# RWKV attention and a mixture of experts on one core: sends one step sooner, two more units transposed by TensorE, blank rows from ScalarE's queue

## Chip, cores and metric

One core of a Trainium2 chip. The metric is the device time of one launch, in microseconds, as the median of several runs. TensorE multiplies matrices, VectorE and ScalarE work on tiles, GpSimd does products between tiles in SBUF and issues indirect DMAs, and SyncE (SP) issues most of the plain DMAs and all transposing ones. Each engine works through its own instructions in order.

## The reference

Two parts, the second on the output of the first:

```python
for t in range(S):                     # batch 4, heads 8, S 768, head_dim 48
    kt, vt, rt = (k[:, :, t], v[:, :, t], r[:, :, t])
    cur = np.einsum('bhd,bhe->bhde', u[None] * kt, vt)
    y[:, :, t] = np.einsum('bhd,bhde->bhe', rt, state + cur)
    state = w[None, :, :, None] * state + np.einsum('bhd,bhe->bhde', kt, vt)
...
x = y.transpose(0, 2, 1, 3).reshape(3072, 384)
logits = x @ w_gate + modality_bias[modality_id]      # 8 experts
e_idx = np.argmax(logits, axis=1)
gate_w = softmax(logits)[np.arange(N), e_idx]
for e in range(8):
    mask = e_idx == e
    out[mask] = gate_w[mask, None] * (np.maximum(x[mask] @ w1[e], 0.0) @ w2[e])
```

w1 is 384 x 1024 for each expert, w2 is 1024 x 384. Every token goes to one expert.

## The kernel before

**Units and steps.** The attention is cut into 24 units of 128 tokens (4 batches by 6 chunks of the sequence). Step i of the big loop in `run` (L1239) does the attention of unit i and prepares its neighbours: `scores` of unit i + 1 (r times k, L451), `values` of unit i (L479, L486) with the state's update (L501), `token`, `factor`, `high` and `low` of unit i - 1 (the output as a pair of 16-bit halves in the tile `row`), and the keys (`kc`), decays (`rc`), `kt` and r-times-k products (`rk`, from unit 14 on `ru`) of units i + 2 and i + 3. In the code, VectorE's `keys` writes `kc`, GpSimd's `decay` writes `rc` (L377), `carry` writes `kt` (L384), `own_keys` writes `ru` (L390, L391); VectorE's `taken` sums `ru` at the unit's own step (L422).

**Routing.** Units form seven groups (`GROUPS`: 0 to 3, 4 to 7, 8 to 11, 12 to 15, 16 to 18, 19 to 21, 22 and 23). For each group: the rows are transposed (`flip`) into `xT`; two steps after the group's last unit `logits` multiplies them by the gate (six matmuls for each unit, L591); `choose` takes the expert, `count` and `place` give each token a row in its expert's region of the DRAM table `rows`, and `send` writes the rows there with one indirect DMA for each unit (L681, with a one-element memset before each). `choose`, `place` and `ahead` are generators that are worked off a piece at a time wherever the loop calls `fill`. `route(i, d, f)` calls f for the group whose last unit is d steps back.

**Transposing.** `flip` has two ways. For units 0 to 7 (`TURNED`) and for the last, TensorE transposes six 128 x 128 tiles into PSUM (L577) and ScalarE copies them to `xT` (`flipped`, L581). For the others SP issues a transposing DMA (L572), and TensorE waits for it at the logits.

**Slots.** The expert that is expected to be the fullest is begun while the attention runs: ten slots of 128 rows of it. `turn` reads a slot's rows from `rows` with a transposing DMA into `mxT` (L1027) and a small one (L1028); it waits for every send that was issued before it. `s_up` multiplies by w1 (`phs`, L1040), `s_high` and `s_low` make the 16-bit halves `hh` and `hl`, `s_down` multiplies by w2 (`pos`, L1114, L1119), `s_take` and `s_give` write the result. In the loop, slots 0 to 5 go up at steps 11, 13, 15, 17, 19 and 21 (`ups`) and down one step later; their turns are issued at the end of steps 9, 10, 13, 14, 17 and 18, turns 6 and 7 at the end of steps 21 and 22 (`turns`). Slots 6 to 9 follow after the loop in an order written out by hand. After the slots a loop goes through the other experts' rows.

**Blank rows.** `fronts` (L298) writes 128 rows of zeros at the front of each expert's region, 1544 KB in one DMA. It is called at the end of step 22, ahead of turn 7, and issued by SP.

**PSUM.** `scores`, the transposes of `flip`, `s_up` and `s_down` take tiles in turn from one ring of four (`ps_a`).

**Order on GpSimd.** In each step: `send` of two units of the group six steps back, `own_keys`, `decay`, `send` of two more, `s_give`, `carry`, `sign` (L1309 to L1317). SP's order in a step: the loads of k and v (L357), r (L365) and of the transposed r and k (L348) for later units, then `flip`, then a piece of the second expert's weights (L942) or a `turn`.

Of the kernel before, what the change touches and what calls it, by code (L numbers as in the profile page):

```python
# [45 lines left out]

TURNED = 7

# [16 lines left out]
class _Kernel:  # L65
# [225 lines left out]

    def blank(self, rows, of):
        i = self.nc.sync.dma_start(rows, of)
        self.tc.add_to_no_dep_group("rows", i.ins)
        self.tc.declare_no_dep(i.ins, group="rows", reason="every row has a place of its own")
        self.tc.declare_no_dep(i.ins, group="read", reason="rows that are there before")

    def fronts(self):  # L298
        self.blank(self.rows[: E * CAP].rearrange("(e p) w -> p e w", e=E)[:P], self.pad.unsqueeze(1).to_broadcast([P, E, RW]))

# [268 lines left out]
    def flip(self, i, by_dma=True):  # L569
        nc, u = self.nc, self.ctx_[i]  # L570
        if by_dma:
            nc.sync.dma_start_transpose(u["g"]["xT"][:, u["at_g"], :, :], u["x16"])  # L572
            return
        early = i <= TURNED
        u["pt"] = (self.ps_a if early else self.ps_s).tile([P, 2 * DC, P], F16, tag="big" if early else "s", name=f"pt{i}")
        for q in range(2 * DC):
            nc.tensor.transpose(u["pt"][:, q, :], u["x16"][:, q * P : (q + 1) * P], self.id16)  # L577
# [549 lines left out]
    def run(self):  # L1127
# [26 lines left out]
        def plan(step, f):  # L1154
            at.setdefault(step, []).append(f)
# [28 lines left out]
        plan(9, self.wide_u)  # L1184
        plan(22, self.fronts)
        second = lambda q: lambda: piece(1, q)
# [34 lines left out]
        def each(i, *fs):  # L1221
            for f in fs:
                if live(i):
                    f(i)
# [14 lines left out]
        for i in range(NU - 1):  # L1239
# [3 lines left out]
            if i:  # L1243
                each(i + 1, self.scores)
            if 0 <= i - 2 <= TURNED:
                self.flip(i - 2, False)
# [5 lines left out]
            first = i <= BARE  # L1252
            self.token(i - 1) if i else None
            if i == 12:
                fine(4)()
# [10 lines left out]
            if first:  # L1266
# [7 lines left out]
                each(i - 1, self.high)  # L1274
                if 0 <= i - 2 <= TURNED:
                    self.flipped(i - 2)
# [22 lines left out]
            if down is not None:  # L1299
# [3 lines left out]
                if down == 0:  # L1303
                    fine(5)()
            late = i >= NU - 3
            if not first:
                each(i + 2, self.keys)
                each(i + 5, lambda i: self.turned(i, both=True))
            for k in range(2):  # L1309
                route(i, 6, self.send, 2, True)  # L1310
                if k == 0:
                    each(i + 2, self.own_keys)
                    each(i + 3, self.decay)
            if ups.get(i - 2) is not None:
                self.s_give(ups[i - 2])
            each(i + 2, self.carry)
            route(i, 4, self.sign)  # L1317
            if not first:
                for _ in self.factor(i - 1):
                    fill()  # L1320
                self.own(i, 0)
                each(i - 1, self.high)
                for j in range(2):
                    each(i + 1, lambda i: self.causal(i, j))
                    fill()
                self.own(i, 1)
                each(i - 1, self.low)
                fill()
            if i - 1 > TURNED:
                self.flip(i - 1)  # L1330
# [18 lines left out]
            route(i, 2, self.logits)  # L1349
            if late:  # L1350
                route(i, 5, self.send, B, True)
            for f in at.get(i, ()):
# [47 lines left out]
        run(c5, 9)  # L1400
        self.s_take(6)
        self.s_up(7, 0)
        self.logits(g6, self.ps_s, "s")
# [180 lines left out]
```

## Time and profile before

| | |
|---|---|
| median of 3 runs | 345.27 us (344.1 to 346.49) |
| the profiled execution | 345.37 us, span 343.6 us |
| TensorE busy | 322.0 us, 94% of the span |
| VectorE busy | 223.2 us, 65% |
| GpSimd busy | 167.2 us, 49% |
| ScalarE busy | 158.5 us, 46% |

The span is the stretch from the first to the last recorded instruction; times in rows count from its start. A busy TensorE means that matmuls are in its pipeline, so that two neighbouring rows can overlap by their last tenth of a microsecond. In a timeline, the brackets behind a row give the idle time of the engine just before it and what ended it; instructions of one kind that follow each other are one row, with their count.

### The profile page before, as it was taken

The numbers are of one execution on the slowest core, as the hardware profiler recorded it, in microseconds if no ns is written. First come the engines' busy times: TensorE is split into PE (matmuls) and PEld (weight loads), VectorE is DVE, ScalarE is ACT, GpSimd is POOL, SyncE is SP. The second block draws the span as 40 slices with busy tenths as digits, with TensorE's granted clock in tenths as the row PEclk, the third lists the DMA queues.
The fourth block names the chain that finished last, engine by engine and source line by source line (L and its number), as shares of the span: only waits on it lengthen the run. The fifth ranks groups of instructions, "written<-read, shape, count | busy, mean of one in ns | idle before, by whom it ended". The sixth has DMA issues, their size and how long they took to land. (4 is left out here: it accounts for less than half of the span.)

```text
span 343.6 us, 14756 instructions
## 1 busy us (share of the span) xinstructions
PE 322.0 (94%) x5371; PEld 259.4 (75%) x5371; DVE 223.2 (65%) x735; ACT 158.5 (46%) x378; POOL 167.2 (49%) x261
## 2 busy tenths in 40 slices
PE   6899999999869998999897999999999999999992
PEld 2778888797867886879687777776788888877771
DVE  6898789988768677888764853358333334437960
ACT  5756677472527573647732222265222222227820
POOL 8997688924777498678621721111111121111321
PEclk9999999999989998999999999999999999999999
DMA  6989899999997999699574331217932111211110
GB/s 142 250 210 279 201 256 242 199 147 192 255 251 155 193 271 260 197 197 222 147 248 94 125 87 50 47 46 234 206 67 48 46 46 46 68 47 46 36 46 4
DMA packets 56093, 50.69 MB, mean 148 GB/s; under 512 B 40936, under 2 KB 49641, under 8 KB 55792
## 3 DMA queue, kind: packets, MB, share of 16 engines
q1 hardware_dynamic: 51888, 37.85, 51.4%
q0 software_dynamic: 3200, 9.47, 7.4%
q10 hardware_dynamic: 960, 2.75, 3.2%
q8 instruction: 31, 0.51, 0.7%
q14 instruction: 14, 0.11, 0.1%
HBM read 30.55 MB, written 11.63 MB: 123 GB/s over the span
## 5 line engine op out<-in xcount | busy, mean ns | idle before, releaser
L1040 PEld LDWEIGHTS <-whi 128*128 128x128 f16 x1248 | 72.6, 98 | 7.8 <-issue 3.6
L1114 PEld LDWEIGHTS <-hh 128*128 128x128 f16 x416 | 39.1, 98 | 25.1 <-ACT hh L1044 0.9
L1040 PE MATMUL phb<-mxT,whi 128*128 128x128 f16 x720 | 47.5, 219 | 0.4 <-DVE mt L1464 0.4
L377 POOL TENSOR_TENSOR rc<-ud,powr 128x512 f32<-128x512 f32 (+1 forms) x27 | 33.1, 1231 | 10.3 <-DMA ud<-in_pd 10.1
L1040 PEld LDWEIGHTS <-wlo 128*128 128x128 f16 x624 | 37.7, 98 | 0.0
L1044 ACT ACTIVATE hh<-phb 128x256 f16<-128x256 f32 (+1 forms) x45 | 20.3, 452 | 34.8 <-PE phb L1040 25.2
L1040 PE MATMUL phs<-mxT,whi 128*128 128x128 f16 x480 | 30.1, 219 | 3.8 <-DMA mxT<-rows 3.7
L457 DVE TENSOR_TENSOR at<-psc,mask 128x512 f32<-128x512 f32 x48 | 31.5, 680 | 0.1
L1119 PEld LDWEIGHTS <-hl 128*128 128x128 f16 x208 | 19.9, 98 | 15.1 <-issue 2.5
L1009 POOL TENSOR_TENSOR seenb<-otb,putb 128x1 int32<-128x1 int32 x15 | 3.8, 256 | 55.2 <-ACTq L1506 47.7
L681 POOL DMA_INDIRECT rows<-row,posi x24 | 25.1, 1046 | 10.9 <-DVE pr L791 5.1
L451 PE MATMUL psc<-rc,kc 48*64 48x128 f32 x768 | 28.3, 284 | 1.6 <-DVE kc L401 1.5
L1114 PE MATMUL po<-whi,hh 128*128 128x384 f16 x128 | 28.7, 326 | 0.2
L1114 PE MATMUL po<-wlo,hh 128*128 128x384 f16 x128 | 28.6, 326 | 0.1
L1049 DVE SCALAR_TENSOR_TENSOR hl<-phb,hh 128x256 f16<-128x256 f32 (+1 forms) x45 | 22.6, 512 | 7.6 <-ACT hh L1044 4.7
L486 PE MATMUL py<-kv,at 128*64 128x48 f32 x768 | 27.3, 225 | 0.3 <-DMA kv<-in_pt 0.3
L1040 PE MATMUL phb<-mxT,wlo 128*128 128x128 f16 x360 | 27.4, 219 | 0.0
L1000 ACT ACTIVATE otb<-po,fac 128x384 f32<-128x384 f32 x15 | 8.7, 580 | 40.5 <-PE phb L1040 36.7
L1124 DVE TENSOR_SCALAR fac<-mt,wf 128x1 f32<-128x1 f32 x16 | 3.4, 213 | 36.7 <-ACTq L1506 28.0
L486 PEld LDWEIGHTS py<-kv,at 128*64 128x64 f32 x768 | 26.1, 142 | 0.7 <-DVE at L457 0.3
L563 ACT ACTIVATE row<-py,sx 128x384 f16<-128x384 f32 x24 | 13.9, 579 | 27.5 <-DVE sx L327 18.4
L451 PEld LDWEIGHTS psc<-rc,kc 48*64 48x64 f32 x768 | 21.7, 136 | 5.0 <-POOL rc L377 3.0
(275 smaller groups left out, 664.3 us busy)
## 6 DMA issues: line engine op xcount, KB each, us to landing
kv<-in_pt SPq DMA_DIRECT2D x24, 384.0 KB, 5.7
ud<-in_pd SPq DMA_DIRECT2D x34, 192.0 KB, 6.0
raw<-in_w SPq DMA_DIRECT2D x12, 512.0 KB
raw<-in_w SPq DMA_DIRECT2D x2, 1536.0 KB, 7.6
ud<-in_pd ACTq DMA_DIRECT2D x14, 192.0 KB
r<-in_pt SPq DMA_DIRECT2D x10, 192.0 KB, 6.9
rows<-pad SPq DMA_DIRECT2D x1, 1544.0 KB
rows<-row,posi POOLq DMA_INDIRECT x24, 5.1
```

What stands on the lines that cost most here:

```text
L377: nc.gpsimd.tensor_mul(u["rc"][:, s], u["rT"][:, s], self.powr[:, s])
L451: nc.tensor.matmul(u["ps"][j][s, pr * P : (pr + 1) * P], u["kc"][r, pr, s], u["rc"][r, pr, :], start=True, stop=True)
L457: return nc.vector.tensor_mul(u["at"][:, j * NPR : (j + 1) * NPR, :], u["ps"][j].rearrange("p (q t) -> p q t", q=NPR), self.mask.unsqueeze ...
L486: nc.tensor.matmul(py[t, sl], u["at"][:, j * NPR + pr, t], u["v"][:, sl], start=c == h == 0, stop=h == H - 1 and i >= BARE, skip_group_che ...
L563: self.nc.scalar.activation(u["x16"][:, :DM], u["x"], AF.Copy, scale=u["g"]["sx"][:, b : b + 1])
L681: i = nc.gpsimd.indirect_dma_start(out=self.rows, out_offset=bass.IndirectOffsetOnAxis(ap=u["posi"][:, b : b + 1], axis=0), in_=u["row"][: ...
L1000: self.nc.scalar.activation(ot, po[:, :DM], AF.Copy, scale=gf[:, t : t + 1])
L1040: self.nc.tensor.matmul(ph[:, q * P : (q + 1) * P], w[:, c0 : c0 + P], self.xT[:, xq, t * P : (t + 1) * P], start=i == q == 0, stop=i == l ...
L1044: self.nc.scalar.activation(self.hh[:, f0 : f0 + fb, t * P : (t + 1) * P], p3, AF.Relu)
L1049: self.nc.vector.scalar_tensor_tensor(self.hl[:, f0 : f0 + fb, r], p3, 0.0, self.hh[:, f0 : f0 + fb, r], ALU.max, ALU.subtract)
L1114: self.nc.tensor.matmul(po[:, :DM], self.hh[:, f, t * P : (t + 1) * P], w[:, c0 : c0 + DM], start=n == 0, stop=False)
L1119: self.nc.tensor.matmul(po[:, :DM], self.hl[:, f, t * P : (t + 1) * P], self.whi[:, c0 : c0 + DM], start=False, stop=f == FB - 1)
```

## The change

Four edits, which belong together:

- `TURNED` becomes a list of units: 0 to 7, and now 11 and 15. These two, each the last of its group, are transposed by TensorE at the beginning of steps 13 and 17, and ScalarE copies them behind `high`. SP no longer issues their transposing DMAs.
- From step 12 on, the four sends of a group come one step sooner, five steps behind the group's last unit instead of six, and their place among GpSimd's products changes: `decay`, one send, `carry`, the other sends, then `own_keys` (r's products last), `s_give`. Up to step 11 the order is: one send, `own_keys`, `decay`, the remaining sends, `carry`, and two sends of the group five steps back.
- For this, `fill(4)` runs the first four pieces of `place`, up to the positions `posi`, at the head of that step.
- `fronts` is issued by ScalarE's queue, after slot 6 has been taken, and no longer by SP ahead of turn 7.

```diff
-TURNED = 7
+TURNED = (*range(8), 11, 15)
...
-    def blank(self, rows, of):
-        i = self.nc.sync.dma_start(rows, of)
+    def blank(self, rows, of, queue=None):
+        i = (queue or self.nc.sync).dma_start(rows, of)
...
-        early = i <= TURNED
+        early = i in TURNED
         u["pt"] = (self.ps_a if early else self.ps_s).tile([P, 2 * DC, P], F16, tag="big" if early else "s", name=f"pt{i}")
...
-        plan(22, self.fronts)
...
+            if not first and any(hi + 4 == i for lo, hi in GROUPS):
+                fill(4)
...
-            for k in range(2):
-                route(i, 6, self.send, 2, True)
-                if k == 0:
-                    each(i + 2, self.own_keys)
-                    each(i + 3, self.decay)
-            if ups.get(i - 2) is not None:
-                self.s_give(ups[i - 2])
-            each(i + 2, self.carry)
+            if first:
+                route(i, 6, self.send, 1, True)
+                each(i + 2, self.own_keys)
+                each(i + 3, self.decay)
+                route(i, 6, self.send, B, True)
+                each(i + 2, self.carry)
+                route(i, 5, self.send, 2, True)
+            else:
+                each(i + 3, self.decay)
+                route(i, 5, self.send, 1, True)
+                each(i + 2, self.carry)
+                route(i, 5, self.send, B, True)
+                each(i + 2, self.own_keys)
+                if ups.get(i - 2) is not None:
+                    self.s_give(ups[i - 2])
...
                 each(i - 1, self.high)
+                if i - 2 in TURNED:
+                    self.flipped(i - 2)
...
-            if i - 1 > TURNED:
+            if i and i - 1 not in TURNED:
                 self.flip(i - 1)
...
         self.s_take(6)
+        self.fronts()
         self.s_up(7, 0)
```

TensorE's instructions at step 13 before: `psc` are the scores of unit 14, `py` the values of unit 13, `phs` slot 1.

```order
L451 MATMUL psc_1_1945<-rc_1640,kc_1834 64x128
L479 MATMUL py_2008<-st_94,rc_1512 64x96 x8
L486 MATMUL py_2008<-kv_1485,at_1851 64x48 x16
L501 MATMUL pst_2033<-kv_1485,kt_90 48x48 x8
L1040 LDWEIGHTS whi
```

And now, from the sixth of the six new pairs on (`row` holds unit 11's halves, `pt` is its PSUM tile):

```order
L577 LDWEIGHTS row_1332
L577 MATMUL pt_1969<-id_149,row_1332 128x128
L479 MATMUL py_2015<-st_94,rc_1512 64x96 x8
L486 MATMUL py_2015<-kv_1485,at_1865 64x48 x16
L501 MATMUL pst_2040<-kv_1485,kt_90 48x48 x8
L1040 LDWEIGHTS whi
```

Six such pairs stand between the scores and the values; nothing else moved there.

GpSimd's instructions in steps 12 and 13 before: `row_801` and `posi` are the group of units 4 to 7, `ru` units 14 and 15, `rc` units 15 and 16.

```order
L390 TENSOR_TENSOR ru_1838<-r_1595,kv_1516 128x384
L391 TENSOR_TENSOR ru_1838<-ru_1838,ub 128x384
L377 TENSOR_TENSOR rc_1841<-ud_88,powr 128x512
L384 TENSOR_TENSOR kt_91<-kv_1516,wtok 128x384
L680 MEMSET gap 1x1
L681 DMA rows<-row_801,posi_1846 25856x772
L680 MEMSET gap 1x1
L681 DMA rows<-row_801,posi_1846 25856x772
L390 TENSOR_TENSOR ru_1982<-r_1797,kv_1593 128x384
L391 TENSOR_TENSOR ru_1982<-ru_1982,ub 128x384
L377 TENSOR_TENSOR rc_1985<-ud_85,powr 128x512
L680 MEMSET gap 1x1
```

And now, from the same place:

```order
L377 TENSOR_TENSOR rc_1843<-ud_88,powr 128x512
L680 MEMSET gap 1x1
L681 DMA rows<-row_801,posi_1823 25856x772
L384 TENSOR_TENSOR kt_91<-kv_1516,wtok 128x384
L680 MEMSET gap 1x1
L681 DMA rows<-row_801,posi_1823 25856x772
L680 MEMSET gap 1x1
L681 DMA rows<-row_801,posi_1823 25856x772
L680 MEMSET gap 1x1
L681 DMA rows<-row_801,posi_1823 25856x772
L390 TENSOR_TENSOR ru_1854<-r_1595,kv_1516 128x384
L391 TENSOR_TENSOR ru_1854<-ru_1854,ub 128x384
```

All four sends now stand behind the first `rc` and ahead of the first `ru`; before, the last two stood behind the second `rc`.

SP's instructions at the end of step 22 before: the transposing DMA of unit 21, the blank rows, and turn 7.

```order
L572 DMA_TRANSPOSE xT_3226<-row_3225 128x6x128
L293 DMA rows<-pad 128x8x772
L1071 TENSOR_LOAD ctl
L1071 ISA x2
L1027 ISA
L1027 DMA_TRANSPOSE mxT<-rows 128x6x128
L1028 ISA
L1028 DMA mt_301<-rows 128x4
```

And now:

```order
L572 DMA_TRANSPOSE xT_3240<-row_3239 128x6x128
L1071 TENSOR_LOAD ctl
L1071 ISA x2
L1027 ISA
L1027 DMA_TRANSPOSE mxT<-rows 128x6x128
L1028 ISA
L1028 DMA mt_301<-rows 128x4
```

The DMA of the blank rows is gone from between them; it stands on ScalarE between slot 6's result (L1000) and slot 7's first `hh` (L1044).

## Rows read from the trace of the kernel before

**Rows 1.** TensorE's waits, whole span: line, who, us in total, times, longest.

```profile
PE pr L591 <- DMA xT<-row: 5.5, 2, 3.9
PE phs L1040 <- DMA mxT<-rows: 3.7, 4, 1.4
```

**Rows 2.** Timeline of TensorE, steps 13 to 18: start, length, instruction, count.

```profile
85.50 1.10 PE L451 MATMUL psc<-rc,kc 48*64 48x128 f32 x32
...
92.73 0.60 PE L591 MATMUL pr<-wghl,xT 128*128 128x16 f16 x18
97.20 0.30 PE L591 MATMUL pr<-wghl,xT 128*128 128x16 f16 x6 [3.88 <-DMA xT<-row]
97.44 1.88 PE L451 MATMUL psc<-rc,kc 48*64 48x128 f32 x32
...
106.17 1.10 PE L451 MATMUL psc<-rc,kc 48*64 48x128 f32 x32
...
114.13 1.10 PE L451 MATMUL psc<-rc,kc 48*64 48x128 f32 x32
...
121.26 1.10 PE L451 MATMUL psc<-rc,kc 48*64 48x128 f32 x32
...
128.42 0.83 PE L591 MATMUL pr<-wghl,xT 128*128 128x16 f16 x18
...
131.12 1.45 PE L451 MATMUL psc<-rc,kc 48*64 48x128 f32 x32
...
139.82 1.10 PE L451 MATMUL psc<-rc,kc 48*64 48x128 f32 x32
```

**Rows 3.** Windows: length, each engine's busy time, granted clock, DMA share, GB/s.

```profile
93.00:96.00 3.00, 0.33 (x14) 0.23 (x10) 0.00 (x0) 2.06 (x6) 1.37 (x2) 1.00 1.39 98
99.00:102.00 3.00, 3.00 (x70) 2.75 (x64) 2.97 (x10) 0.60 (x2) 2.46 (x5) 0.66 1.06 301
```

**Rows 4.** Timeline of TensorE, first products of slots 2, 6, 7 and 8.

```profile
110.02 1.50 PE L1040 MATMUL phs<-mxT,whi 128*128 128x128 f16 x24 [0.30 <-DMA mxT<-rows]
...
170.25 1.51 PE L1040 MATMUL phs<-mxT,whi 128*128 128x128 f16 x24 [1.41 <-DMA mxT<-rows]
...
182.16 1.50 PE L1040 MATMUL phs<-mxT,whi 128*128 128x128 f16 x24 [1.20 <-DMA mxT<-rows]
...
187.57 1.50 PE L1040 MATMUL phs<-mxT,whi 128*128 128x128 f16 x24 [0.77 <-DMA mxT<-rows]
```

**Rows 5.** Timeline of TensorE: one unit's transposes, one group's logits, earlier steps.

```profile
58.09 0.51 PE L577 MATMUL pt<-id,row 128*128 128x128 f16 x6
...
62.33 0.76 PE L591 MATMUL pr<-wghl,xT 128*128 128x16 f16 x24
```

**Rows 6.** Timeline of VectorE: unit 11's low half, the masks of unit 14.

```profile
84.12 0.61 DVE L567 SCALAR_TENSOR_TENSOR row<-py,sx,row 128x384 f16<-128x384 f32 x1
...
89.84 1.29 DVE L457 TENSOR_TENSOR at<-psc,mask 128x512 f32<-128x512 f32 x2
```

**Rows 7.** Timeline of ScalarE: `high` of unit 12; `flipped` of the last unit.

```profile
89.90 0.58 ACT L563 ACTIVATE row<-py,sx 128x384 f16<-128x384 f32 x1 [1.79 <-DVE sx L327]
...
179.78 0.78 ACT L581 COPY xT<-pt 128x768 f16<-128x768 f16 x1
```

**Rows 8.** Waits of SP's DMA queue, whole span.

```profile
SPq L1027 <- DMA rows<-row,posi: 30.9, 5, 8.7
...
SPq L1027 <- DMA rows<-pad: 7.2, 1, 7.2
```

**Rows 9.** Timeline of SP's DMA queue: turn 2, the blank rows.

```profile
106.96 1.25 SPq L1027 DMA_TRANSPOSE mxT<-rows  x1
...
170.37 0.57 SPq L293 DMA_DIRECT2D rows<-pad  x1
```

**Rows 10.** Timeline of GpSimd: `ru` of unit 14, a send of group 4 to 7.

```profile
86.93 1.01 POOL L390 TENSOR_TENSOR ru<-r,kv 128x384 f32<-128x384 f32 x1 [4.19 <-PE psc L451]
...
91.83 1.02 POOL L681 DMA_INDIRECT rows<-row,posi  x1 [0.16 <-issue]
```

More of the change, by code (lines that the diff above doesn't have):

```diff
@@ L298, in fronts @@
     def fronts(self):
-        self.blank(self.rows[: E * CAP].rearrange("(e p) w -> p e w", e=E)[:P], self.pad.unsqueeze(1).to_broadcast([P, E, RW]))
+        self.blank(self.rows[: E * CAP].rearrange("(e p) w -> p e w", e=E)[:P], self.pad.unsqueeze(1).to_broadcast([P, E, RW]), self.nc.scalar)
     def setup3(self):
@@ L1244, in run @@
                 each(i + 1, self.scores)
-            if 0 <= i - 2 <= TURNED:
+            if i - 2 in TURNED:
                 self.flip(i - 2, False)
@@ L1274, in run @@
                 each(i - 1, self.high)
-                if 0 <= i - 2 <= TURNED:
+                if i - 2 in TURNED:
                     self.flipped(i - 2)
@@ L1304, in run @@
                     fine(5)()
-            late = i >= NU - 3
             if not first:
@@ L1322, in run @@
                 each(i - 1, self.high)
+                if i - 2 in TURNED:
+                    self.flipped(i - 2)
                 for j in range(2):
@@ L1349, in run @@
             route(i, 2, self.logits)
-            if late:
-                route(i, 5, self.send, B, True)
             for f in at.get(i, ()):
```

## The prediction

> **What bounds the kernel now.** The page's first part gives TensorE 94% of the span, so I ask first where its missing microseconds lie. TensorE's own waits [rows 1] name two causes with several microseconds each: the logits product `pr` waits twice for `xT` (the DMA transposes of `flip`), 5.5 us in all and 3.9 in one; the slots' product `phs` waits four times for `mxT` (the DMA transposes of `turn`), 3.7 us. The timeline of TensorE says when. Call a step the stretch from one `scores` product (L451) to the next. In step 13 [rows 2] the logits start at 92.73, do 18 of 24 matmuls, those of units 8 to 10, and stand 3.88 us until unit 11 is there. Step 17 is the same with units 12 to 15 (5.5 less 3.88 leaves 1.6). What follows a stop is slow: step 14 goes from 97.44 to 106.17, 8.73 us, while step 16, with the same instructions (scores, values, one slot's down half), goes from 114.13 to 121.26, 7.13; step 18, from 131.12 to 139.82, takes 8.70. [...] The four waits of `phs` are 0.30 at slot 2, then 1.41, 1.20 and 0.77 at slots 6, 7 and 8 [rows 4].
>
> **Units 11 and 15 on TensorE.** Each flip adds six matmuls into a PSUM tile: six take 0.51 us where the kernel already does it [rows 5]. 24 logits without a stop take 0.76 [rows 5]. Step 13 becomes 92.73 - 85.50 = 7.23, plus 0.51, plus 0.76: 8.50 instead of 11.94 (97.44 - 85.50). Saved: 3.44. Step 17 becomes 128.42 - 121.26 = 7.16, plus 1.27: 8.43 instead of 9.86. Saved: 1.43. With no stop, steps 14 and 18 should take step 16's 7.13: saved 1.60 and 1.57. Call these four A to D, for units 11 and 15 and the steps behind them: together 8.04.
>
> Are the operands there? TensorE reaches the new transposes after `scores`, one microsecond into step 13, at 86.5; VectorE writes the low half of unit 11 at 84.12 for 0.61 [rows 6], so 1.8 us early. The new tile takes a turn in the ring of four PSUM buffers, so that the second half of the slot's up product now takes the buffer of `psc` 14's first half: VectorE masks both halves from 89.84 in 1.29 [rows 6], the first by some 90.5, and TensorE wants the buffer near 91.2 (92.73 less 2.0 for the 36 matmuls of the second half, 24 taking 1.5 by [rows 4], plus 0.51). Cover 0.7; without it, up to that much per flip. ScalarE copies the tile out, 0.78 [rows 7], behind `high` of unit 12 (89.90, for 0.58) [rows 7]: done at 91.3, and unit 11's six logits matmuls come no sooner than 93.2 (92.73 plus 0.51). It costs nothing as long as ScalarE runs less than two microseconds late.
>
> **Sends sooner.** A `turn` waits for every send written before it, and SP issues in order: SP stood 30.9 us at five turns for `rows<-row,posi` and 7.2 for `rows<-pad` [rows 8]. Turn 2 went out at 106.96 [rows 9] and slot 2 started at 110.02 [rows 4]. This is the part without which the first would be lost: TensorE now reaches slot 2 by 3.44 + 1.60 sooner, at 104.7 and not 109.7, and with turn 2 at 106.96 would stand there until 110.02. The change puts the four sends of units 4 to 7 one step earlier, right behind `rc`, with the positions worked out first on VectorE. Before, GpSimd stood until 86.93 for `ru`, I think for its late load of r (the product that the row names does not feed it), then did the sends from 91.83 on [rows 10], two at a time. Now: one product `rc` (512 columns where `ru` has 384 in 1.01, so some 1.3), four sends of 1.02 and a memset, some 1.3 each, one `kt`, then two of `ru`, 1.0 each: 9.5 us. From 82.7, where that wait of 4.19 began, the last send ends near 90.2 and `ru` near 92.2; VectorE wants `ru` of unit 14 only behind the logits, near 94.0 (85.50 + 8.50). If `rc` could not start before 86.93, `ru` would end at 96.4, 2.4 late. So the cost is between nothing and 2.4; I take nothing, because the loads of `rc` are asked for before the late load of r. Turn 2 then leaves by 98 to 99 instead of 107 and SP's loads behind it do too; the 0.30 goes. The later groups move in the same way: turn 6 leaves with its sends one step older, so slot 6's 1.41 goes.
>
> **Blank rows on ScalarE's queue.** Turn 7 stood 7.2 us behind the blank rows on SP [rows 8], and unit 22's transpose and turn 8 stood behind turn 7. That is slot 7's 1.20 and slot 8's 0.77. The DMA is now issued after slot 6 is taken, 0.57 us of issue by its row on SP [rows 9], on an engine that next waits for TensorE anyway. Of what is late next I see turn 9: it waits for the sends of units 19 to 21, whose positions hang behind slot 7's result, which comes sooner by 1.41 + 1.20 and not by the 0.77 too; and now for the blank rows. So between 0 and 0.77 comes back; I take 0.4.
>
> [...]
>
> **Sum.** 8.04 + 0.30 + 1.41 + 1.20 + 0.77 - 0.4 = 11.3. The profiled execution took 345.37 around a span of 343.6, the median of the three runs is 345.27, so nothing has to be corrected: 345.3 - 11.3 = 334.0. After the slots TensorE has no gap, and nothing there is changed.
>
> **Rivals.** *The transfers become the bound.* DMA shares of 1.39 and 1.06 [rows 3] leave little room, and TensorE now asks for the same bytes in 8 us less. If nothing could come sooner but what two dropped transposes free, A to D shrink to those: in the window with transposes 98 GB/s were moved, in the one without 301, so 0.29 MB in 3 us, and a transpose of 0.2 MB is some 2 us. 4 + 3.4 at slots 6 to 8: 338.0. Against it: SP stood still for most of 30.9 us [rows 8] before its turns, with the loads of the next units behind it, and can now ask for them sooner.
>
> [...]
>
> *Units 10 and 14 are late instead.* They still go by DMA. They had landed when the first 18 logits ran. Now four sends of 0.2 MB lie beside them, 0.8 MB or 2.6 us at 301 GB/s. Two stops of up to 2.6, with part of the slow clock: 340.
>
> *The sends don't come sooner.* If VectorE's positions are late, turns 2 and 4 leave when they did, TensorE stands 5 to 8 us at slots 2 and 4, and A to D are gone: 345.3 less 1.2 to 3.4, 343.
>
> *The blank rows collide.* They now run in the stretch before turn 9. If the transfer lasts beyond the sends, turn 9 is late by what is left, at most the 7.2 us that SP saw: 341. That needs the DMA to begin only when turn 9 is due, and it is issued a slot's up and down products earlier; a part of it is likelier, and is counted with the first rival.
>
> *GpSimd becomes the bound (slower).* Four sends, 5.1 us, now stand ahead of `ru`; VectorE works in order, and its sum over `ru` comes before the masks and the low halves on which TensorE waits. If at each of the three groups this block came onto the path, that is 15.3 us against 11.3 of gain, 349. It decides once GpSimd is more than a step behind. For it: its sends now wait for VectorE's positions with all of a step's products behind them. Against it: `ru` is wanted two steps after its place, and the order puts `rc`, wanted by `scores`, first.
>
> **How the numbers follow.** Forecast 0.66 with its own range 332 to 336.5; transfers or the blank rows 0.17 (336.5 to 340); units 10 and 14 late 0.07; sends not sooner 0.05; GpSimd 0.05. Differences under 1%, 3.4 us, count as none, about what a measurement of this kernel tells apart. Faster: 0.66 + 0.17 + 0.06 = 0.89; same: 0.01 + 0.05 = 0.06; slower 0.05. The range goes from 331.5 (nothing comes back, and some waits of other engines go too) to 339.5, which takes in most of the first rival.
>
> **What would show it.** Right: no wait of `pr` for `xT`; granted clock 1.00 from 90 to 140; steps 14 and 18 near 7.1; `phs` waiting under 1 us in all; turn 2 issued before 100. Wrong: a wait of TensorE for `mxT` at slot 2 or 4 (sends), for `xT` again (units 10, 14), for `hh`, `at` or `dv` behind a VectorE that waits for `ru` (GpSimd), or at slot 9 (blank rows). If the waits go and steps 14 and 18 still take 8.7, the slow clock was not theirs.

## The result, and the profile after

The changed kernel took 342.01 us, median of 11 runs (338.96 to 344.19), where the kernel before took 344.74 beside it: a ratio of 0.9896, interval 0.9847 to 0.9945. That is 1.0% or some 3.6 us faster, where 334.0 and a range of 331.5 to 339.5 were predicted. Medians here are over all runs of a kernel; ratios leave disturbed runs out. Later groups of runs, each on one chip, gave 340.6 to 342.5 for the same kernel in two of them and 356 in two others, where it is 2.1 and 2.8% slower than the kernel before. So there are two questions: where 7.7 of the predicted 11.3 us went, and why the gain turns into a loss elsewhere.

The profiled execution took 339.3 us, its span is 337.6. TensorE's waits, whole span (line, who, us in total, times, longest), against [rows 1]:

```profile
PE py L486 <- issue: 2.7, 2, 1.9
...
PE pr L643 <- DVE row L634: 1.1, 1, 1.1
```

Both causes of [rows 1] are gone: no `pr` waits for `xT`, no `phs` for `mxT`. New are 2.7 us of the values product (`py`) put down to "issue": TensorE stood there and waited for nothing that the profile shows. The timeline of TensorE, steps 13 to 15, against [rows 2]:

```profile
88.21 1.10 PE L451 MATMUL psc<-rc,kc 48*64 48x128 f32 x32
89.25 0.51 PE L577 MATMUL pt<-id,row 128*128 128x128 f16 x6
...
96.75 0.75 PE L591 MATMUL pr<-wghl,xT 128*128 128x16 f16 x24
97.43 1.10 PE L451 MATMUL psc<-rc,kc 48*64 48x128 f32 x32
...
102.13 0.26 PE L486 MATMUL py<-kv,at 128*64 128x48 f32 x2 [1.87 <-issue]
...
106.76 1.10 PE L451 MATMUL psc<-rc,kc 48*64 48x128 f32 x32
...
111.38 0.24 PE L643 MATMUL pr<-oh,warm 128*128 128x8 f16 x4 [1.14 <-DVE row L634]
...
115.77 1.10 PE L451 MATMUL psc<-rc,kc 48*64 48x128 f32 x32
```

The flip takes its 0.51 and the 24 logits run without a stop. Step 13 is 97.43 - 88.21 = 9.22, step 14 is 9.33 and not 7.13, step 15 is 9.01. In step 14 TensorE has done 30 of 32 `py` matmuls, stands 1.87 us, and does the last two. The windows, against [rows 3], with one from the start:

```profile
20.00:30.00 10.00, 10.00 (x181) 8.49 (x181) 6.44 (x27) 3.21 (x8) 6.02 (x6) 0.66 0.49 137
...
93.00:96.00 3.00, 2.83 (x49) 2.55 (x47) 2.93 (x7) 2.10 (x5) 2.92 (x3) 1.00 1.07 314
99.00:102.00 3.00, 1.26 (x40) 1.13 (x35) 2.97 (x5) 0.24 (x2) 2.33 (x4) 1.00 1.32 219
```

The granted clock between 99 and 102 is 1.00 where it was 0.66, as predicted; yet TensorE works 1.26 of 3 us there. The first row is this execution's own loss: from 16.5 to 26.7 us, part of steps 1 and 2, the granted clock was 0.50, though the code there is the same as before, and TensorE came to unit 14's scores at 88.21 and not at 85.50. SP's queue, its wait for the sends, against [rows 8], and then turn 2 in its timeline, against [rows 9]:

```profile
SPq L1027 <- DMA rows<-row,posi: 7.2, 2, 4.3
```

```profile
98.86 2.02 SPq L1027 DMA_TRANSPOSE mxT<-rows  x1
```

30.9 us at five turns became 7.2 at two, and turn 2 left at 98.86, in the 98 to 99 that was foreseen, though this execution had lost 2.7 us ahead of it.

### The profile page after: what moved, and what is told of

It reads as the page before. It is cut to its first block, busy times and chain, and to the rows that moved or that the text cites. A ratio compares the mean times of both kernels' runs of the same rounds, so it can differ in the third digit from the quotient of the medians.

```text
span 337.6 us, 14775 instructions
## 1 busy us (share of the span) xinstructions
PE 322.9 (96%) x5383; PEld 260.1 (77%) x5383; DVE 227.6 (67%) x735; ACT 160.5 (48%) x380; POOL 167.5 (50%) x261
## 5 line engine op out<-in xcount | busy, mean ns | idle before, releaser
L1044 ACT ACTIVATE hh<-phb 128x256 f16<-128x256 f32 (+1 forms) x45 | 20.3, 452 | 34.3 <-PE phb L1040 20.4
L1000 ACT ACTIVATE otb<-po,fac 128x384 f32<-128x384 f32 x15 | 8.7, 580 | 40.4 <-PE phb L1040 40.0
```

The source lines that it names most:

```text
L1000: self.nc.scalar.activation(ot, po[:, :DM], AF.Copy, scale=gf[:, t : t + 1])
L1044: self.nc.scalar.activation(self.hh[:, f0 : f0 + fb, t * P : (t + 1) * P], p3, AF.Relu)
```

## The experiments

**First group: the parts alone, and the change again.** `te_only` is the kernel before with `TURNED = (*range(8), 11, 15)` and the line that copies behind `high`; `sends_only` has the new order of sends and products with `fill(4)`; `blank_only` has `fronts` on ScalarE's queue.

> Only the two flips move to TensorE; sends, order of GpSimd's products and blank rows as before. Theories for the whole study: P (GpSimd's products now run back to back and hold up VectorE's kc, which lets TensorE wait in steps 13 to 15), S (the profiled execution of the changed kernel lost some 3 us to a slow clock in its first 30 us, which is not the change's), D (more transfers in a shorter time hold TensorE up at the values product). By the prediction's terms: step 13 takes 8.5, but turn 2 still leaves near 107, so TensorE reaches slot 2 near 105 and stands there for about 5 us; steps 17 and 18 give 3.0 less what turn 4 is late. Time 342 to 345. P: kc under 1.7 us in steps 13 to 15, since GpSimd's order is the old one. D: a wait at the values product (L486) of over 1 us in step 14 is possible only if the transfers crowd, and turn 2 isn't sooner here, so none.

> Only the sends one step sooner and the new order of GpSimd's products. By the prediction's terms: the stop at unit 11's transpose stays (step 13 near 11.9 or more, as its DMA now has the sends beside it), turn 2 leaves before 100, slot 2's wait of 0.3 and slot 6's of 1.4 go: 343 to 344. P: kc over 2 us in one of steps 13 to 15, as in the changed kernel, but TensorE's stop at xT hides part of it, so the time is 343 to 346. S and D say nothing here.

> Only the blank rows move to ScalarE's queue behind slot 6. By the prediction's terms slot 7's wait of 1.20 and slot 8's of 0.77 go and up to 0.77 comes back at turn 9: 1.2 to 2.0 sooner, 343.3 to 344.1. If the 1.5 MB collide with turn 9: no gain or up to 2 us slower. P and D: no change before slot 6.

> The changed kernel once more, unaltered. S: a profile with a granted clock of 1.00 in the first 30 us has step 12's scores near 78 and not 80.65, and a time near 336 to 337; one with the slow stretch has 339 to 340. P: kc of over 2 us in step 13 or 14 and steps 13 to 15 of 27 to 28 us together, whatever the clock at the start. D: the wait of 1.9 us at the values product in step 14 comes again at the same place.

Medians 344.55, 343.92, 346.24 and 342.49 beside 346.6; ratios 0.9954 (0.9914 to 0.9994), 0.9912 (0.987 to 0.9954), 0.9974 (0.9917 to 1.0031), 0.9968 (0.9911 to 1.0025). As medians over all runs the parts come to 2.1, 2.7 and 0.4 us and the whole to 4.1. By the ratios they come to 0.5, 0.9 and 0.3% and the whole to 0.3%, each with an interval of about half a per cent to either side, so whether the parts add up is not shown. `blank_only` fell short of the 1.2 to 2.0 us that were expected of it. TensorE's timeline in `te_only`:

```profile
84.47 1.10 PE L451 MATMUL psc<-rc,kc 48*64 48x128 f32 x32
...
92.75 1.10 PE L451 MATMUL psc<-rc,kc 48*64 48x128 f32 x32
...
97.49 0.26 PE L486 MATMUL py<-kv,at 128*64 128x48 f32 x2 [1.91 <-issue]
...
102.11 1.10 PE L451 MATMUL psc<-rc,kc 48*64 48x128 f32 x32
...
108.14 1.50 PE L1040 MATMUL phs<-mxT,whi 128*128 128x128 f16 x24 [2.46 <-DMA mxT<-rows]
```

Step 13 takes 8.28: the prediction's 8.50. Step 14 takes 9.36 with the same stop at the same two matmuls as the changed kernel, though sends and products keep their old order; D had expected none here, and so falls in the form that ties it to turn 2. In `after_again` it is 1.32 us, again at the last two matmuls.

S, the slow start that is not the change's, held in part. `after_again` had a slow stretch at the start too (0.66 from 15 to 30 us), came to unit 14's scores at 92.43 and took 342.66. The others of this group came there at 84.47, 88.48 and 94.45, and `base3`, the kernel before once more (fourth group), at 88.31 with a clock of 0.89 from 15 to 30 us. So a late start is no part of the change; it costs 3 to 9 us in some executions. The clock is not all of it: in `sends_only` it is 1.00 up to 85 us, and of the 6.9 us in `after_again` 4.0 are stops of the kind that follows. In `after_again` `kc` of step 14 took 0.74 and step 15 7.52.

What is the stop? Count TensorE's records from the first (weight loads, matmuls, its semaphores). The stops of over 0.5 us for "issue" in this group stand at 450, 1474, 2242, 2498, 4034, 4290, 4802, 5314 and 5826: all 194 + 256k. The list of DMA queues has a queue q8 of kind instruction: 31 packets, 0.51 MB, 16 KB each. Up to 200 us there is one such packet for each stretch of 256 records. So I take it that TensorE's program comes in pieces of 256 instructions, and call this F. Record 4290 is the 31st `py` matmul of step 14 where the flip of unit 11 stands ahead, and twelve records further, in the state's update, where it does not.

The table has what each trace shows there (runs of the later groups too), in us after TensorE passed record 4034. The stop at `xT` lies between the two records; the upper five traces have the old flips. "Stood" is counted from the start of the record before, 0.2 more than the idle time:

```
              stop at xT   q8 packet      stood at 4290   went on after its landing
before          3.9        6.5 to 7.6     0.0             2.5
sends_only      3.6        5.6 to 6.7     0.0             3.3
base3           1.2        5.2 to 6.3     2.0             1.5
blank_only      none       3.7 to 5.1     2.0             1.4
before_last     none       5.2 to 6.3     3.1             1.3
te_only         none       4.3 to 5.3     2.1             1.5
after           none       4.0 to 5.1     2.1             1.7
after_again     none       3.8 to 4.9     1.5             1.4
control3        none       3.9 to 5.0     1.8             1.5
kept_sends      none       4.6 to 5.7     2.2             1.3
pieces_late     none       1.9 to 3.3     0.0             1.5
```

Wherever TensorE stood, it went on 1.3 to 1.7 us after the packet had landed; without a stop it needs 4.8 us from record 4034 to 4290 (`pieces_late`). The first five rows show more than the changed kernel does: where the stop at `xT` is long there is none at 4290, and where it is short or missing the old flips have the stop at 4290 too. The one wait covers the other. TensorE in `base3`, steps 13 and 14:

```profile
98.36 0.30 PE L591 MATMUL pr<-wghl,xT 128*128 128x16 f16 x6 [1.21 <-DMA xT<-row]
...
103.32 0.47 PE L501 MATMUL pst<-kv,kt 128*48 128x48 f32 x12 [1.80 <-issue]
```

In `after` the packets between 17 and 82 us begin 0.3 to 2.3 us after TensorE has entered the piece before, and the two of step 13 4.2 and 4.0 us after; when a packet is asked for is in no trace. DMA queues of `control3` in 93.1:97.0, which begins at record 4034, and in 96.9:98.2:

```profile
q1 hardware_dynamic: 547, 1.14, 83.6%
q0 software_dynamic: 74, 0.20, 19.4%
...
q1 hardware_dynamic: 156, 0.34, 105.8%
q8 instruction: 1, 0.02, 5.4%
```

In the first stretch the two queues together use 103% of the engines' time and no q8 packet begins; in the second it does, with queue q1 alone at 105.8%. So in this trace the load by itself does not decide when the packet goes. At one record of the series TensorE stood 4.1 us (`sends_only`, record 5314).

**Second group: move the stop.**

```diff
-        for _ in range(WARM):
-            nc.tensor.matmul(pt, self.ones16, warm, start=True, stop=True)
+        for _ in range(75):
+            nc.tensor.matmul(pt[:, :P], self.ones16, warm[:, :P], start=True, stop=True)
```

> The changed kernel, but the 11 wide warming matmuls at the start are 75 of 128 columns: the same 4.7 us of work, 128 more TensorE instructions ahead of everything. New theory F: TensorE gets its instructions in pieces of 256 (16 KB, queue q8 in the list of DMA queues), asks for the next piece when it begins one, and stands where that piece has not landed; so far each wait of over 0.5 us put down to 'issue' after the first steps stands at record 194 + 256k of TensorE, and goes on 1.3 to 1.7 us after a q8 packet has landed. Rival D': the wait at the values product of step 14 (1.9, 1.9 and 1.3 us in three profiles) belongs to that product, by an operand or by the transfers beside it. F: the waits stay at 194 + 256k, which are now other instructions: none at the values product of step 14; the pieces there are begun 7.7, 6.5 and 7.5 us apart and not 6.6 and 4.8, so no wait over 0.6 us in steps 13 to 15, step 14 takes 7.1 to 7.7, time 1 to 2 us below the changed kernel's. D': step 14 still takes 8.7 to 9.4 with the wait at the 31st matmul of the values product.

For `pieces_late` and `pieces_last` (third group) the second expert's weights are asked for later:

```diff
-            plan(11 + 4 * (q // 2) + q % 2, second(q))
-            plan(13 + 4 * (q // 2) + q % 2, norm(q))
+            plan(15 + q, second(q))
+            plan(17 + q, norm(q))
```

That is `pieces_late`; in `pieces_last` they stand at `plan(min(18 + q, 22), second(q))`, the first three are squared two steps later and the last three behind slot 6. `give_first` puts the call of `s_give` ahead of `own_keys`.

> The changed kernel, but the six 512 KB pieces of the second expert's weights are asked for at the end of steps 15 to 20 (and squared two steps later), instead of 11, 12, 15, 16, 19 and 20. F (TensorE's next instructions come late because transfers crowd them out): with 1 MB less asked for ahead of steps 12 to 14 the q8 packets there begin under 3 us after TensorE has begun the piece before, not 4.0, and the wait of step 14 falls under 1 us; steps 16 to 20 have more to move and one of them gains a wait. Time between 2 us below and 1 us above the changed kernel's. D' in its form of an operand: step 14's wait stays at 1.3 to 2.1 us.

> The changed kernel, but GpSimd writes a slot's result (s_give) ahead of own_keys and not behind it. P (VectorE's kc stands still beside GpSimd's products; 4.14 us in one profile of the changed kernel, 0.74 in the other): the four products of step 14 no longer stand in a row of 4.6 us, kc takes under 2.2 us in steps 13 to 15, step 15 takes 7.5 to 7.9, and the wait of the count's product stays under 0.3. Time: 0 to 1.2 us below the changed kernel's; F's waits are untouched, so step 14 still takes 8.7 to 9.4.

Medians 353.79, 352.88 and 353.19 beside 348.47 (ratios 1.0196, 1.0176, 1.018): all three slower than before by about the same amount. The changed kernel itself was not in this group, so the times say nothing of the edits. The traces do. In `shift128` the stops are still at 194 + 256k (450, 2498, 3778, 4290, 5570; a second kind follows below), and 4290 is now in the scores of step 14; `py` there runs through:

```profile
101.56 0.81 PE L451 MATMUL psc<-rc,kc 48*64 48x128 f32 x18 [0.61 <-issue]
102.30 0.88 PE L479 MATMUL py<-st,rc 112*64 112x96 f32 x16
103.01 1.09 PE L486 MATMUL py<-kv,at 128*64 128x48 f32 x32
```

F holds and D' falls: the stop belongs to the record's number, not to the product. F's sizes were off: step 13 took 9.00 and step 14 8.12. (The warming took 5.78 us in place of 4.75, not the same, which the numbering does not depend on.) In `pieces_late` the packet began 1.9 us after record 4034, the stop was 0.03 and step 14 took 7.30; but pieces 5314 and 5570 then came 0.75 and 3.12 late and step 18 took 10.24, so the stop was moved, not removed. In `give_first` `kc` stayed at 1.27 or less in steps 13 to 15 and step 15 took 7.56, as P has it; step 14 took 8.79.

**Third group: why slower here.** `control2` is the changed kernel, `last_give` is `pieces_last` with `s_give` ahead of `own_keys`.

> The changed kernel unaltered, on the chip of the next two runs: what they are compared with. The three runs of shift128, pieces_late and give_first were all 4 to 6 us slower than the kernel before on their chip, whatever their edit, so the chip itself may set whether the change gains. F: the sum of TensorE's waits at records 194 + 256k up to 200 us is 4 to 8 us, the largest in steps 13 to 18, and the time against the kernel before follows that sum. If the change is slower than before here too, the chips differ; if it is 1 to 1.2% faster, the three edits themselves cost.

> The changed kernel, but the second expert's six 512 KB pieces are asked for at the end of steps 18 to 22 (two at 22), and the last three squared after slot 6: nothing of them lies beside steps 12 to 18. F: q8 packets in steps 12 to 17 begin under 3.5 us after TensorE has begun the piece before; no wait over 1 us at 194 + 256k between 90 and 140; steps 14 and 18 take 7.1 to 7.6; the sum of these waits falls by 2 to 4 us against control2, and the time by 1.5 to 3 us. Rival (the crowding is by transposes and sends, or the memory of the chip): the sum stays within 1 us of control2's.

> pieces_last, and GpSimd writes a slot's result ahead of own_keys. F and P together: as pieces_last, and kc at most 1.7 us in steps 12 to 16, no wait for the count; 0 to 1 us below pieces_last. If P is worth nothing on the path: the same as pieces_last.

Medians 356.31, 355.25 and 358.11 beside 347.63; `control2`'s ratio is 1.0276 (1.0209 to 1.0342). The change itself is slower here, and again in the fifth group. I call these groups the second kind, the others the first. The kernel before is a little slower in them too, 347.6 to 349.2 for 344.7 to 346.6. F doesn't explain it: the stops at 194 + 256k in `control2` are only 1.7 us up to 200 us. Step 20 takes 13.24, where the first profile has 7.21. TensorE in step 20 of `control2`:

```profile
145.49 1.10 PE L451 MATMUL psc<-rc,kc 48*64 48x128 f32 x32
...
148.30 0.28 PE L479 MATMUL py<-st,rc 112*64 112x96 f32 x1 [0.43 <-issue]
...
149.04 0.38 PE L486 MATMUL py<-kv,at 128*64 128x48 f32 x4 [0.46 <-issue]
149.78 0.47 PE L486 MATMUL py<-kv,at 128*64 128x48 f32 x3 [0.36 <-issue]
150.53 0.24 PE L486 MATMUL py<-kv,at 128*64 128x48 f32 x1 [0.29 <-issue]
151.25 1.52 PE L486 MATMUL py<-kv,at 128*64 128x48 f32 x23 [0.47 <-issue]
...
158.73 1.10 PE L451 MATMUL psc<-rc,kc 48*64 48x128 f32 x32
```

GpSimd at the same time:

```profile
145.49 1.02 POOL L681 DMA_INDIRECT rows<-row,posi  x1 [0.16 <-POOL gap L680]
...
146.81 0.98 POOL L681 DMA_INDIRECT rows<-row,posi  x1 [0.21 <-issue]
...
148.09 0.98 POOL L681 DMA_INDIRECT rows<-row,posi  x1 [0.21 <-DMA r<-in_pt]
...
149.37 0.97 POOL L681 DMA_INDIRECT rows<-row,posi  x1 [0.21 <-issue]
```

And the window behind it:

```profile
151.30:157.00 5.70, 5.70 (x40) 3.52 (x41) 3.24 (x12) 0.58 (x2) 1.06 (x2) 0.59 0.52 135
```

While four sends go out in a row, TensorE's instructions come a few at a time, every 0.74 us; I call this batches. Behind it, from 151.3 to 157, the granted clock is 0.59. All six traces of these two groups show such batches beside the four sends of step 20 and the three at slot 6 (there a single stop of 0.4 in `shift128` and `last_give`), four of them also in step 13, and five near 60 us. The traces of the first group show none, beside four sends in a row either: away from the records 194 + 256k they have no stop of over 0.2 us for "issue" up to 205 us. That it is the supply of instructions that stutters is read from the stops, for which the profile names no cause; nothing was run to test it. The traced execution of `control2` is the fastest of its six, 349.21; why the others took 355 to 361 is in no trace. `pieces_last` took 8.28 and 7.13 in steps 13 and 14, the prediction's figures, with the pieces there in time; its median gained only 1 us on `control2`.

**Fourth and fifth groups: is it the row of sends?** `base3` is the kernel before, `control3` and `control4` the changed one, `kept_sends` the changed one with the old sends; `spread` is

```diff
                 each(i + 2, self.carry)
-                route(i, 5, self.send, B, True)
+                route(i, 5, self.send, 1, True)
                 each(i + 2, self.own_keys)
                 if ups.get(i - 2) is not None:
                     self.s_give(ups[i - 2])
+                route(i, 5, self.send, B, True)
```

> The kernel before, unaltered, traced on the chip of the next three runs. Theory G, from six traces on two chips on which the changed kernel was 2.0 to 2.8% slower than the kernel before: there, while GpSimd issues three or four sends in a row, TensorE gets its instructions in batches (a few matmuls, then 0.3 to 0.5 us of 'issue', again every 0.7 us); on the two chips where it was 1.0 to 1.2% faster its four traces show none of that. G, on a chip of the slow kind: the kernel before, whose sends stand two by two, shows no such batches outside its rows of three or five sends, and step 20 takes 7 to 8 us. On a chip of the other kind: none in any of these four runs.

> The changed kernel, unaltered, on the same chip as base3. G, on a chip of the slow kind: batches in step 12 or 13, step 20 and at slot 6 (each beside three or four sends), step 20 of 11 to 14 us with a granted clock of 0.5 behind it, 2 to 3% slower than base3. On a chip of the other kind: no batches, 1 to 1.3% faster than base3.

> The changed kernel, but only one send stands behind kt and the last two behind own_keys and s_give: no three sends in a row before the loop's end. Turn 2 waits for the last send; in the changed kernel's first profile that had 6 us in hand, so no wait at slot 2. G, on a chip of the slow kind: the batches in steps 12, 13 and 20 go, 5 to 9 us sooner than control3. If instead the number of sends within a step counts: as control3. On a chip of the other kind: as control3 within 1 us.

> The kernel before with units 11 and 15 on TensorE and the blank rows on ScalarE's queue, but the sends and GpSimd's order as before. G, on a chip of the slow kind: no batches in steps 12 to 22; 5 to 9 us sooner than control3 and 0.3 to 0.8% faster than base3. On a chip of the other kind: 0.5 to 0.8% faster than base3 (the two parts alone gave 0.6 and 0.1% in medians), 1.5 to 2 us behind control3, most of it at slot 2.

Medians 346.43, 340.57, 342.5 and 342.38 beside 345.14; ratios 1.0041 (1.0 to 1.0082), 0.9908 (0.9868 to 0.9947), 0.9878 (0.9784 to 0.9971), 0.9906 (0.9853 to 0.9959). No batches in any of the four: the group is of the first kind and left G (the row of sends causes the batches) open. `spread` is level with `control3` by the ratios, 1.9 us behind it as medians where 1 was expected. `control3`, traced in the fastest of its 12 runs, is the cleanest trace of the changed kernel, its clock 1.00 throughout, 337.87 us. It has `kc` of step 14 at 4.07 us, as `after` has it at 4.14. Timeline of VectorE and then of GpSimd:

```profile
98.33 4.07 DVE L401 TENSOR_TENSOR kc<-ud,powk 128x512 f32<-128x512 f32 x1
...
98.68 1.26 POOL L377 TENSOR_TENSOR rc<-ud,powr 128x512 f32<-128x512 f32 x1
99.90 0.99 POOL L384 TENSOR_TENSOR kt<-kv,wtok 128x384 f32<-128x384 f32 x1
100.86 0.99 POOL L390 TENSOR_TENSOR ru<-r,kv 128x384 f32<-128x384 f32 x1
101.93 1.33 POOL L391 TENSOR_TENSOR ru<-ru,ub 128x384 f32<-128x384 f32 x1
```

`kc` begins 0.35 us ahead of four GpSimd products in a row and ends in the last; only that one is slowed, by 0.33. `base3`, with `kc` at 0.68, and `after_again`, at 0.74, took 7.5 us for step 15, `control3` 9.03 and `after` 9.01, with 0.96 and 1.14 us of wait for the count. In `spread` `kc` is 0.68 and step 15 takes 7.53.

> The changed kernel, unaltered, for comparison with the next three. On a chip of the kind of control3: no batches beside the sends, the wait of 1.3 to 2.1 us at record 4290 in step 14 again, 0.9 to 1.3% faster than before. On a chip of the kind of control2: batches beside three or four sends in a row, step 20 of 11 to 14 us, 2 to 3% slower than before.

> pieces_last again (the second expert's weights asked for in steps 18 to 22), on this chip. F: step 14 takes 7.1 to 7.6 and step 13 8.3 to 8.7, with no wait over 0.4 us at record 4290; 1.5 to 3.5 us sooner than control4. Rival (it was only that chip's chance): step 14 takes 8.7 to 9.4 and the time is control4's within 1 us.

> pieces_last4 and spread together. On a chip of the kind of control3: as pieces_last4 within 1 us. On a chip of the kind of control2, by G: no batches in steps 12, 13 and 20, step 20 takes 7.2 to 8, and 5 to 9 us sooner than pieces_last4; if the row of sends isn't the cause, the batches stay.

> The kernel before with the second expert's weights asked for in steps 18 to 22. F and the prediction's own terms: TensorE's stop in step 13 is set by unit 11's transpose, which may land up to 1.5 us sooner with 1 MB less beside it; 0.5 to 2 us sooner than the kernel before, so that most of what pieces_last4 gains over control4 isn't to be had without the change. If it gains 3 us or more, the move of the weights is worth the same with and without the change.

Medians 355.71, 355.08, 349.51 and 351.79 beside 349.24; ratios 1.0212 (1.0153 to 1.0271), 1.0204 (1.0127 to 1.0282), 1.0057 (1.0021 to 1.0093), 1.0117 (1.0064 to 1.0171). This group is of the second kind. `last_spread` has the same edits as `pieces_last4` but for the row of sends, and is 5.6 us sooner, in the 5 to 9 of G; step 20 at 8.72 is above its 7.2 to 8. TensorE and then GpSimd in its step 20:

```profile
152.25 0.30 PE L479 MATMUL py<-st,rc 112*64 112x96 f32 x2 [0.46 <-issue]
152.98 0.32 PE L479 MATMUL py<-st,rc 112*64 112x96 f32 x2 [0.42 <-issue]
...
153.18 1.12 PE L486 MATMUL py<-kv,at 128*64 128x48 f32 x30
...
158.66 1.10 PE L451 MATMUL psc<-rc,kc 48*64 48x128 f32 x32
...
149.94 1.01 POOL L681 DMA_INDIRECT rows<-row,posi  x1 [0.16 <-POOL gap L680]
...
151.25 0.98 POOL L681 DMA_INDIRECT rows<-row,posi  x1 [0.21 <-issue]
```

Two sends leave two short stops, step 20 takes 8.72 and not 13.69 (`pieces_last4`), and the batches that `pieces_last4` has in steps 13 and 16 are gone. Those near 60 us, where `spread` changes nothing, stay. The stops of over 0.2 us for "issue" away from 194 + 256k, up to 205 us, add up to 8.0 us in `control4` and in `pieces_last4`, 3.4 in `last_spread` and 2.0 in `before_last`, whose sends stand two by two as in the kernel before and whose step 20 takes 7.25. So the row of sends costs some 6 us here. Moving the weights is worth nothing: `pieces_last4` again stood 1.83 us at 4290 and equals `control4`, and `before_last` is 1.2% slower than before where 0.5 to 2 us of gain were expected. That `pieces_last` had its pieces in time was this execution's chance. What exactly keeps the q8 packet waiting, the transposes, the sends or the loads of k, v and r, was not tried apart. Nor is it known what makes a group of the second kind; the second and the fourth group report the same chip number, so it is not shown to be the chip.

## Why the prediction was wrong

- *Units 11 and 15: C right, A right by itself and mis-sized in the whole.* Step 13 took 8.28 in `te_only`, 8.27 in `kept_sends` and 8.28 in `pieces_last`, for 8.50; step 17 took 8.28 in `after`, `after_again`, `control3` and `kept_sends`, for 8.43. In the changed kernel itself step 13 takes 9.2 to 9.3. In `after` and `control3` GpSimd's products lie beside `kc` (1.94 us), VectorE's state and masks are late (waits of 0.19 to 0.25 and of 0.17), and the PSUM cover of 0.7 is used up; in `after_again`, with `kc` at 0.69, it is 0.81 of "issue" at record 4034. What was saved was smaller than A has it for another reason too: the stop of 3.88 was one execution's. The same transpose held the logits for 3.58 in `sends_only`, 1.21 in `base3`, and not at all in `blank_only` and `before_last`.
- *The steps behind, B: this failed.* "With no stop, steps 14 and 18 should take step 16's 7.13." Step 14 took 8.8 to 9.4 with the clock at 1.00 in `after`, `after_again`, `te_only` and `control3`. In the trace that the prediction read, the stop at `xT` had hidden the late piece of instructions: it landed 7.6 us after record 4034 and TensorE came to record 4290 later still. Without the stop the piece is the next thing that is late, 1.5 to 2.1 us. The prediction's sign for this case, "the slow clock was not theirs", would have misled: the clock of 0.66 [rows 3] did go there. It does not go for good: in `kept_sends` the stops of 2.0 and 2.1 us for "issue" were followed by a clock of 0.85 and 0.84, and steps 14 and 18 took 11.03 and 10.84. D was nearer in `after`, `after_again` and `control3`: 7.36, 7.76 and 7.91 for 7.13.
- *"GpSimd's cost is between nothing and 2.4; I take nothing": mis-sized.* It came by a way that the prediction did not look at: four products in a row beside `kc`, 1.5 us in step 15 in two of three traces of the changed kernel in groups of the first kind. The old order isn't free of it either (3.29 us in `kept_sends`). And the sends in a row, which the prediction counted as time on GpSimd alone, cost some 6 us in a group of the second kind (5.6 between `pieces_last4` and `last_spread`).
- *Slots: right in the sum, not in the split.* No wait of `phs` at slots 6, 7, 8 and 9 in `after`. From unit 23's scores to the end `control3` takes 177.8 and before 181.8: 4.0 saved for 2.98; the 0.4 at turn 9 did not come back. The prediction gave 1.41 to the sends and 1.97 to the place of the blank rows. The traces of the parts say otherwise: `sends_only`, with the blank rows still on SP, has no such wait either and takes 177.6 from there to the end; `blank_only` keeps 1.49 at slot 6 and takes 179.8. With turn 6 gone sooner, SP issues the blank rows 4.9 us behind unit 23's scores and not 8.6. So the sends alone were enough in that one trace.
- *The sum.* `control3`, which has the clock at 1.00 everywhere and starts within 0.4 us of before, gains 345.37 - 337.87 = 7.5 of the 11.3: 4.0 of the 8.3 between unit 14's scores and unit 23's, and 4.0 in the slots. The 4.0 of 8.3, step by step: 2.6 of 3.44 in step 13 (A), -0.3 of 1.60 in step 14 (B), -1.1 of 0.30 in step 15 (slot 2, and the products beside `kc`), 1.6 of 1.43 in step 17 (C), 0.8 of 1.57 in step 18 (D), and 0.4 elsewhere. The median of 340.6 is 2.7 above that execution. And the base was one draw: TensorE's idle time at the records 194 + 256k up to 200 us is 1.1 us in before with 5.5 at `xT`, and 7.6 in `base3` with 1.2 at `xT`, 6.6 and 8.8 together, where the spans differ by 2.0. In the changed kernel's traces of the first kind it is 2.8, 2.9 and 6.7. The change took the stops at `xT` away, and not the pieces that stand in for them.
- *The rivals.* "The transfers become the bound", 338.0, was nearest: TensorE did outrun the transfers, but what came late was its own program and no operand, and to it no wait in the profile of before pointed but 0.6 us of "issue" at one product of step 10. Units 10 and 14 were never late; the sends came sooner as said; the blank rows did not collide. "GpSimd becomes the bound", 349 at a chance of 0.05, names the engine and the direction that the second kind of group shows, by another mechanism: no wait for VectorE, but the sends themselves.

## What to carry to other kernels

Where an engine with many small instructions waits beside full DMA queues, look for what the wait also hides: count its records between the packets of the instruction queue, and see whether the next piece is late once the wait is gone, as it was here by 1.5 to 2.1 us (`te_only`, `after`, `after_again`, `control3`). In this kernel indirect sends that were issued one after another were better put in pairs with products between them: `spread` is level with the changed kernel in a group of the first kind, and in one of the second `last_spread` is 0.6% behind the kernel before where the changed one is 2% behind (`spread` without the moved weights was not run there). One profile is one draw: before a wait of a few us becomes a term of the sum, see in a second profile of the same kernel whether it is there (3.88 in one here, 1.21 in the next).

## What the runs showed of the hardware

- The instruction queue q8 moved 31 packets of 16 KB, up to 200 us one for each 256 of TensorE's records (`after`); with 128 instructions more ahead the stops were still at records 194 + 256k, beside those of the second kind (`shift128`); next to queues at 103% such a packet began 3.9 us after TensorE had entered the piece before (`control3`), and TensorE stood up to 4.1 us (`sends_only`, record 5314).
- In three of six groups of runs, beside three or four indirect sends in a row, TensorE ran a few instructions at a time, every 0.74 us (`control2`); in the others the same program shows none of it (`control3`).
- A VectorE product of two SBUF tiles, `kc`, took 0.68 us beside a send (`base3`, step 14) and 4.07 and 4.14 beside four GpSimd products in a row (`control3`, `after`), of which the last took 1.33 and not 1.00. By the trace of `control3` `kc` had begun 0.35 us before the first of the four, and it ended in the last of them.
